# Attention and MLP on one core: the low parts and padded copies of K and V for the second batch pair, moved to later steps

## The chip, the cores and the metric

The kernel runs on one core of a Trainium2 chip. Times are device microseconds (us) of one execution. Engines by their names in the profile: PE is TensorE (matmuls; PEld its weight loads), DVE VectorE, ACT ScalarE, POOL GpSimd, SP SyncE, whose queue issues all the DMAs named here. Every engine works through its own queue in order; an instruction that waits holds everything behind it.

## The reference

Attention with a learned bias of relative position, then an MLP with squared ReLU. Batch 4, 8 heads, sequence 576, head size 64, float32 throughout:

```
scores = q @ k.T / 8 + bias          # bias[h,i,j] = relu(x*w1 + b1) @ w2,
                                     # x = log1p(|i-j|) / log1p(max(i,1))
attn   = softmax(scores)
y      = attn @ v                    # to 2304 tokens x 512
out    = relu(y @ w_in)**2 @ w_out   # 512 -> 2048 -> 512
```

## The kernel before

**Two halves per number.** TensorE multiplies float16. A float32 operand is split into a high part (its value, scaled by a power of two, rounded to float16) and a low part (what the rounding left over, again float16). A product is the sum of three matmuls: high by high, high by low, low by high.

**Tiling.** The four batches make two pairs (`p` = 0, 1). In a pair the rows of the queries are cut into five chunks (`c`): four of 128 rows of each batch and one, c = 0, of the last 64 rows of both. A step is one pair, chunk and head; the chunks come in the order 0, 3, 2, 4, 1 for the first pair and 1, 4, 2, 3, 0 for the second, with eight heads each, so there are 80 steps and the second pair begins at step 40. Step `t` does, in the program's order: `qk` (scores into PSUM), `softmax_a` (line 441: VectorE adds the bias and takes the row maximum; lines 445 and 447: ScalarE's negated maximum and exponential), `softmax_b` (line 129: ScalarE's cast to the high part; lines 473 and 474: GpSimd subtracts to get the low part; line 476: a transposing DMA `at<-a`), and `pv` (line 506), the product with V of the step three before. The buffers `a` and `at` have two slots each.

**The MLP** is work put between the steps. When a chunk has its eight heads, `finish_x` makes eight units of it. In each, `g1` (line 560) is the first product; ScalarE (line 566), VectorE (568 and 133) and GpSimd (570) make its squared ReLU in two parts; `g2` (line 583) is the second product, two units later. `g2` adds up all eight units in the PSUM tiles `o`, which ScalarE evicts at the end (line 590) before the next chunk's first `g2` can write them.

**K and V.** The tiles of the second pair are loaded and split during steps 31 to 43, while the first pair's last chunk and the second pair's first are computed. A load goes through one of three staging buffers `stg` (the MLP's weights have used them before). `split` then makes the high part on GpSimd (line 131), the low part on VectorE (line 191 for K, line 156 for V, one instruction that reads the staged tile and the high part), for K two ScalarE copies (the last 64 rows of the pair's first batch, the first 64 of its second) into the zero-padded tile `kz` (line 196; `qk` reads it), and for V a GpSimd fill of zeros (line 160). The staging buffer is free when the high and low parts are made; the next load into it (line 179) waits for that in SyncE's queue. Splits are at one a step for steps 32 to 35, two for 36 to 39, one for 40 to 43; in order: K 0 to 3, then K 4, V 0, K 5, V 1, K 6, V 2, K 7, V 3, then V 4 to 7. The K tile of head h is read first at step 40 + h, the V tile at step 43 + h.

**What sets the order.** A planner takes the traced instructions, each with a priority (its place in the program, moved by `place`), simulates the engines, and writes out the order of each engine's queue. An instruction goes into a queue at the first moment at which, in that simulation, the engine is free and its inputs are there; among several, the one traced first. A dependency of the kind `NoSync` only tells the planner to put one instruction behind another on the same engine; it makes no semaphore. `behind()` puts such an edge from everything traced in its block to the engine's last pinned instruction, and `pinned` writes out the order at the start.

Of the kernel before, what the change touches and what calls it, by code (L numbers as in the profile page):

```python
# [51 lines left out]
def tile_attention_moe(  # L52
# [96 lines left out]
    def v_split(p, h, st):  # L149
        t = vp.tile([128, 2, 640], F16, tag="v", name="v")  # L150
        cast(zn("vh", p * 8 + h), t[:, 0, :], st, float(2 ** VS))
        if p == 0:
            cast("P", st, st, float(2 ** VS))
            nc.gpsimd.tensor_tensor(t[:, 1, :], st, t[:, 0, :], op=ALU.subtract)
        else:
            nc.vector.scalar_tensor_tensor(
                out=t[:, 1, :], in0=st, scalar=float(2 ** VS), in1=t[:, 0, :],
                op0=ALU.mult, op1=ALU.subtract)

        nc.gpsimd.memset(t[64:128, 1, :].rearrange("p (b j) -> p b j", b=2)[:, :, 256:320], 0.0)  # L160
        v_t[p, h] = t

    class KV:
        def __init__(self, p, h, which):
# [16 lines left out]
        def split(self):  # L181
            st = self.st
            if self.which == "k":
                n = self.p * 8 + self.h
                t = kp.tile([128, 2, S], F16, tag="k", name="k")
                st = st[:, 0:S]
                cast(zn("kh", n), t[:, 0, :], st, float(2 ** KS))
                if zn("kl", n) == "P":
                    nc.gpsimd.tensor_tensor(t[:, 1, :], st, t[:, 0, :], op=ALU.subtract)
                else:  # L190
                    nc.vector.scalar_tensor_tensor(
                        out=t[:, 1, :], in0=st, scalar=float(2 ** KS), in1=t[:, 0, :],
                        op0=ALU.mult, op1=ALU.subtract)
                for b in range(2):
                    r = slice(64 * b, 64 * b + 64)
                    nc.scalar.activation(out=kz[r, n % NKZ, :, r], in_=t[r, :, 512 - 512 * b:576 - 512 * b], func=AF.Copy)
                k_t[self.p, self.h] = t
            elif self.p:
                v_split(self.p, self.h, st[:, 0:640])
# [198 lines left out]

    st_ = {}
    sums = {}  # L400

    def qk(p, c, h):
        kt = k_t[p, h]
# [25 lines left out]
    def softmax_a(p, c, h):  # L429
# [8 lines left out]
        inv = float(2.0 ** -(QS + KS + 3))  # L438
        for b in range(nb):
            sb = b if c else h % 2  # L440
            nc.vector.tensor_tensor_reduce(  # L441
                s[:, 576 * b:576 * b + 576],
                sc[:, 960 * sb:960 * sb + 576], bt, inv, -3.0e38, ALU.add, ALU.max, mx[:, b:b + 1])
        for b in range(nb):
            nc.scalar.activation(out=nm[:, b:b + 1], in_=mx[:, b:b + 1], func=AF.Identity, scale=-1.0, bias=esc)  # L445
            sl = s[:, 576 * b:576 * b + 576]
            nc.scalar.activation(out=sl, in_=sl, func=AF.Exp, bias=nm[:, b:b + 1], accum_out=su[:, h, b:b + 1])  # L447
        st_[p, c, h] = s

    def softmax_b(p, c, h):  # L450
# [271 lines left out]
            pin[i.engine] = i.name  # L722

    @contextmanager
    def behind():
        cur = nc.cur_bb
        n0 = len(cur.bb.instructions)
        yield
        for i in cur.bb.instructions[n0:]:
            if i.engine in pin:  # L730
                tc.add_manual_dep(i, pin[i.engine], mybir.DependencyInfo(
                    mybir.DependencyClass.NoSync, mybir.DependencyReason.DATA), reason="behind")

    pin = {}
    with pinned():
# [27 lines left out]
        hgen(groups[gi])  # L763
        for h in range(2):
            bias_ld(*steps[h])
    with behind():
        kv_load(0, "v")
        ld_dma(ws)
        kv_load(2, "k")
# [7 lines left out]
    for t in range(NS + LAG):  # L777
        now[0] = t
        fence = ExitStack()
        if t < 2:  # L780
            fence.enter_context(behind())
        last = t - LAG
        if t < NS:
            p, c, h = steps[t]
# [32 lines left out]
        with place("kd"):  # L817
            kv_dma(t + 2)
        w_tasks(t + 1)
        for _ in range(nls[t]):  # L820
            ld_split()
            ld_dma(loads2)
# [53 lines left out]
```

## Time and profile before

| | us |
|---|---|
| three runs | 656.75, 657.12, 660.38 (median 657.12) |
| the profiled execution | 661.45 |
| its span, first to last instruction | 659.7 |
| TensorE (PE) busy | 615.1 (93%) |
| VectorE (DVE) busy | 407.1 (62%) |
| ScalarE (ACT) busy | 388.1 (59%) |
| GpSimd (POOL) busy | 376.5 (57%) |
| mean granted TensorE clock | 0.965 |

Starts in the trace count from the beginning of the span. Busy shares are means over the whole span, so what a stage is bound by is read from its own waits and timeline. Granted clock is a share of full speed. In a row, `out<-in` names the tiles, `L191` the line, `x8` a count; `[4.01 <-POOL v L131]` says that the engine stood idle for 4.01 us before the instruction, and that GpSimd's line 131 ended the wait. The chain of waits follows the last end back, at each step to what released it.

### The profile page before, as it was taken

How to read it: one execution, taken by the hardware profiler on the slowest of the kernel's cores; microseconds unless marked ns; L12 is line 12 of the kernel's file. 1: busy time of each engine (PE TensorE's matmuls, PEld its weight loads, DVE VectorE, ACT ScalarE, POOL GpSimd, SP SyncE). 2: the span in 40 equal slices, each digit the busy share in tenths (PEclk: the TensorE clock that was granted, in tenths of full speed). 3: DMA queues.
4: the chain of work that ended last, by engine and by line, in shares of the span. 5: the costliest groups of instructions: out<-in, count | busy, mean ns of one | idle time of the engine just before them, and what ended most of it. 6: DMA issues, size and time to landing. Idle time of an engine off the chain costs nothing.

```text
span 659.7 us, 15574 instructions
## 1 busy us (share of the span) xinstructions
PE 615.1 (93%) x6056; PEld 394.8 (60%) x6056; DVE 407.1 (62%) x813; ACT 388.1 (59%) x856; POOL 376.5 (57%) x394
## 2 busy tenths in 40 slices
PE   5565798999899999999899999999999999999997
PEld 2223356766455566666576676676676676767664
DVE  7997999888864765585856447346545642632321
ACT  5587978788776476656656655656465564342111
POOL 2757578899665456756775465555464663432221
PEclk9698967999999999999899999999999999999999
DMA  7999888477876787889978778679787777524000
GB/s 237 278 294 319 268 255 248 155 209 178 197 173 152 162 193 176 179 180 226 221 170 158 167 134 174 140 169 153 139 172 134 154 149 155 122 56 86 17 34 16
DMA packets 206568, 112.16 MB, mean 170 GB/s; under 512 B 167072, under 2 KB 183456, under 8 KB 206496
## 3 DMA queue, kind: packets, MB, share of 16 engines
q1 hardware_dynamic: 206496, 111.19, 72.0%
q8 instruction: 47, 0.77, 0.5%
q14 instruction: 25, 0.20, 0.1%
HBM read 55.44 MB, written 15.61 MB: 108 GB/s over the span
## 4 chain that ended last, share of the span: by engine, by line
PE 69%; DVE 5%; DMA 4%; issue 2%; ACT 1%; POOL 1%; DVEq 0%; POOLq 0%; ACTq 0%
PE o L583 26%; PE hp L560 26%; PE pv L506 8%; PE sc L425 5%; PE bp L348 2%; DMA at<-a 2%; DVE hg L309 1%; PE sc L419 1%; PE sc L413 1%; DMA xt<-xh 1%; DMA stg<-vd 1%; DVE s L441 1%; DVE cv L226 0%; DVE ci L224 0%; ACT a L129 0%
## 5 line engine op out<-in xcount | busy, mean ns | idle before, releaser
L560 PE MATMUL hp<-xt,winH 128*128 128x256 f16 (+1 forms) x1280 | 195.9, 263 | 0.0
L583 PE MATMUL o<-woutH,g 128*128 128x512 f16 x576 | 185.6, 382 | 4.0 <-ACT o L590 2.2
L560 PE MATMUL hp<-xt,winL 128*128 128x256 f16 (+1 forms) x640 | 162.8, 263 | 0.0
L583 PEld LDWEIGHTS <-g 128*128 128x128 f16 x864 | 82.8, 98 | 97.0 <-issue 11.5
L560 PEld LDWEIGHTS <-winH 128*128 128x128 f16 x1280 | 117.0, 99 | 30.0 <-issue 13.6
L441 DVE CUSTOM_DVE_ANT_0 s<-sc,bt 128x576 f32<-128x576 f32 x144 | 103.5, 751 | 44.1 <-PE sc L425 34.2
L474 POOL TENSOR_TENSOR a<-s,a 128x1024 f16<-128x1024 f32 (+1 forms) x64 | 130.3, 2036 | 0.0
L568 DVE TENSOR_TENSOR r<-hp,r 128x512 f32<-128x512 f32 (+1 forms) x80 | 50.6, 632 | 118.7 <-ACT r L566 118.6
L570 POOL TENSOR_TENSOR g<-r,g 128x512 f16<-128x512 f32 (+1 forms) x80 | 86.7, 1084 | 59.1 <-DVE g L133 48.4
L447 ACT ACTIVATE s<-s,nm 128x576 f32<-128x576 f32 x144 | 111.3, 773 | 6.4
L583 PE MATMUL o<-woutL,g 128*128 128x512 f16 x288 | 109.8, 381 | 0.0
L473 POOL TENSOR_TENSOR a<-s,a 128x128 f16<-128x128 f32 (+1 forms) x64 | 28.1, 440 | 140.4 <-ACT a L129 135.5
L445 ACT ACTIVATE nm<-mx,esc 128x1 f32<-128x1 f32 x144 | 40.9, 288 | 110.8 <-DVE mx L441 110.5
L506 PE MATMUL pv<-v,at 128*128 128x64 f16 (+5 forms) x2112 | 97.9, 207 | 0.5 <-ACT at L460 0.5
L129 ACT ACTIVATE a<-s 128x1152 f16<-128x1152 f32 (+1 forms) x64 | 70.5, 1102 | 44.6 <-DMA at<-a 43.6
L566 ACT ACTIVATE r<-hp 128x512 f32<-128x512 f32 (+1 forms) x80 | 43.1, 539 | 49.6 <-PE hp L560 49.6
L506 PEld LDWEIGHTS <-at 128*128 128x128 f16 (+1 forms) x1792 | 58.3, 100 | 20.2 <-issue 8.6
L560 PEld LDWEIGHTS <-winL 128*128 128x128 f16 x640 | 62.9, 98 | 5.8
L309 DVE TENSOR_SCALAR hg<-tab_t 128x464 f32<-128x464 f32 (+17 forms) x86 | 58.9, 729 | 11.5 <-PE bp L348 11.4
L425 PE MATMUL sc<-k,q 64*128 64x512 f16 x384 | 55.6, 387 | 0.0
L369 ACT ACTIVATE be<-bp,hcst,rows_s 128x288 f32<-128x288 f32 (+29 forms) x67 | 35.8, 571 | 16.5 <-PE bp L348 11.1
L348 PE MATMUL bp<-hg,w2s 128*32 128x288 f32 (+15 forms) x152 | 36.1, 546 | 6.1 <-ACT hg L303 2.4
(88 smaller groups left out, 688.7 us busy)
## 6 DMA issues: line engine op xcount, KB each, us to landing
bt<-biasd SPq DMA_DIRECT2D x64, 288.0 KB, 3.3
stg<-w_in SPq DMA_DIRECT2D x16, 512.0 KB, 5.1
stg<-w_out SPq DMA_DIRECT2D x16, 512.0 KB, 4.7
bt<-biasd SPq DMA_DIRECT2D x32, 144.0 KB, 3.4
qst<-qd SPq DMA_DIRECT2D x32, 128.0 KB, 3.5
out<-o SPq DMA_DIRECT2D x16, 256.0 KB, 2.4
v<-vd SPq DMA_DIRECT2D x8, 320.0 KB, 4.9
stg<-vd SPq DMA_DIRECT2D x8, 320.0 KB, 4.3
```

The lines of the kernel that those rows point to most:

```text
L129: nc.scalar.activation(out=out, in_=in_, func=AF.Copy, scale=scale)
L309: nc.vector.tensor_scalar(ht, src, scl[:, n:n + 1], None, op0=ALU.min)
L348: nc.tensor.matmul(out=bp[32 * t:32 * t + 32, 0:d1 - d0], lhsT=w2s if gi < 4 or PATS[z][t] == "A" else w2n, rhs=ts_[t][:, d0:d1], start=Tr ...
L425: nc.tensor.matmul(out=sc[:, 1024 * b:1024 * b + 512], lhsT=qt[r, qz, qs], rhs=kt[r, z, 64 * b:64 * b + 512], start=(n == 0), stop=(n == 2 ...
L441: nc.vector.tensor_tensor_reduce(s[:, 576 * b:576 * b + 576], sc[:, 960 * sb:960 * sb + 576], bt, inv, -3.0e38, ALU.add, ALU.max, mx[:, b: ...
L447: nc.scalar.activation(out=sl, in_=sl, func=AF.Exp, bias=nm[:, b:b + 1], accum_out=su[:, h, b:b + 1])
L474: nc.gpsimd.tensor_tensor(av[:, :, 640:1152], ev[:, :, 0:512], av[:, :, 0:512], op=ALU.subtract)
L506: nc.tensor.matmul(out=dst, lhsT=lhsT, rhs=vt[r, 5 * b + blk, :] if f32 else vt[:, vz, 5 * b + blk, :], start=(n == 0), stop=(n == nt - 1) ...
L560: nc.tensor.matmul(out=hp[:, f * T:f * T + T].rearrange("p (b t) -> p b t", b=nb), lhsT=wt[:, k, c0:c0 + 128], rhs=xt[:, 0:nb, z * 4 + k, ...
L568: nc.vector.tensor_tensor(rr, hp[:, 0:2 * T], rr, op=ALU.mult)
L570: nc.gpsimd.tensor_tensor(g[:, 1, 0:2 * T], r[:, 0:2 * T], g[:, 0, 0:2 * T], op=ALU.subtract)
L583: nc.tensor.matmul(out=blk["o"][b], lhsT=g[:, z, c0:c0 + 128], rhs=wt[:, 2 * u + f, :], start=(u == 0 and f == 0 and z == 0 and wt is wout ...
```

## The change

Three moves, for the second pair alone (the first pair's K and V are made as before):

- The low part (lines 191 and 156) isn't traced with the high part. It is put on a list, `lo_due`, with the number of the next step, and traced near the end of that step, with a `NoSync` edge behind the step's softmax maximum on VectorE. V's fill on GpSimd goes with it.
- The two copies into `kz` are put on a list, `kz_due`, two steps on, and are traced there behind the step's last exponential on ScalarE.
- `behind` takes the table of last instructions as an argument; `soft` is the table that `softmax_a` fills with the names of its last maximum and last exponential.

```diff
--- before.py
+++ after.py
@@ -153,12 +153,28 @@
             cast("P", st, st, float(2 ** VS))
             nc.gpsimd.tensor_tensor(t[:, 1, :], st, t[:, 0, :], op=ALU.subtract)
         else:
-            nc.vector.scalar_tensor_tensor(
-                out=t[:, 1, :], in0=st, scalar=float(2 ** VS), in1=t[:, 0, :],
-                op0=ALU.mult, op1=ALU.subtract)
+            lo_due.append((now[0] + 1, t, st, VS))
+            v_t[p, h] = t
+            return
 
         nc.gpsimd.memset(t[64:128, 1, :].rearrange("p (b j) -> p b j", b=2)[:, :, 256:320], 0.0)
         v_t[p, h] = t
+
+    lo_due = deque()
+
+    def low_part(t, st, e):
+        nc.vector.scalar_tensor_tensor(
+            out=t[:, 1, :], in0=st, scalar=float(2 ** e), in1=t[:, 0, :],
+            op0=ALU.mult, op1=ALU.subtract)
+        if e == VS:
+            nc.gpsimd.memset(t[64:128, 1, :].rearrange("p (b j) -> p b j", b=2)[:, :, 256:320], 0.0)
+
+    kz_due = deque()
+
+    def kz_copy(n, t):
+        for b in range(2):
+            r = slice(64 * b, 64 * b + 64)
+            nc.scalar.activation(out=kz[r, n % NKZ, :, r], in_=t[r, :, 512 - 512 * b:576 - 512 * b], func=AF.Copy)
 
     class KV:
         def __init__(self, p, h, which):
@@ -188,12 +204,11 @@
                 if zn("kl", n) == "P":
                     nc.gpsimd.tensor_tensor(t[:, 1, :], st, t[:, 0, :], op=ALU.subtract)
                 else:
-                    nc.vector.scalar_tensor_tensor(
-                        out=t[:, 1, :], in0=st, scalar=float(2 ** KS), in1=t[:, 0, :],
-                        op0=ALU.mult, op1=ALU.subtract)
-                for b in range(2):
-                    r = slice(64 * b, 64 * b + 64)
-                    nc.scalar.activation(out=kz[r, n % NKZ, :, r], in_=t[r, :, 512 - 512 * b:576 - 512 * b], func=AF.Copy)
+                    lo_due.append((now[0] + 1, t, st, KS))
+                if self.p:
+                    kz_due.append((now[0] + 2, n, t))
+                else:
+                    kz_copy(n, t)
                 k_t[self.p, self.h] = t
             elif self.p:
                 v_split(self.p, self.h, st[:, 0:640])
@@ -398,6 +413,7 @@
 
     st_ = {}
     sums = {}
+    soft = {}
 
     def qk(p, c, h):
         kt = k_t[p, h]
@@ -438,13 +454,15 @@
         inv = float(2.0 ** -(QS + KS + 3))
         for b in range(nb):
             sb = b if c else h % 2
-            nc.vector.tensor_tensor_reduce(
+            i = nc.vector.tensor_tensor_reduce(
                 s[:, 576 * b:576 * b + 576],
                 sc[:, 960 * sb:960 * sb + 576], bt, inv, -3.0e38, ALU.add, ALU.max, mx[:, b:b + 1])
+            soft[i.ins.engine] = i.ins.name
         for b in range(nb):
             nc.scalar.activation(out=nm[:, b:b + 1], in_=mx[:, b:b + 1], func=AF.Identity, scale=-1.0, bias=esc)
             sl = s[:, 576 * b:576 * b + 576]
-            nc.scalar.activation(out=sl, in_=sl, func=AF.Exp, bias=nm[:, b:b + 1], accum_out=su[:, h, b:b + 1])
+            i = nc.scalar.activation(out=sl, in_=sl, func=AF.Exp, bias=nm[:, b:b + 1], accum_out=su[:, h, b:b + 1])
+            soft[i.ins.engine] = i.ins.name
         st_[p, c, h] = s
 
     def softmax_b(p, c, h):
@@ -722,13 +740,13 @@
             pin[i.engine] = i.name
 
     @contextmanager
-    def behind():
+    def behind(last):
         cur = nc.cur_bb
         n0 = len(cur.bb.instructions)
         yield
         for i in cur.bb.instructions[n0:]:
-            if i.engine in pin:
-                tc.add_manual_dep(i, pin[i.engine], mybir.DependencyInfo(
+            if i.engine in last:
+                tc.add_manual_dep(i, last[i.engine], mybir.DependencyInfo(
                     mybir.DependencyClass.NoSync, mybir.DependencyReason.DATA), reason="behind")
 
     pin = {}
@@ -763,7 +781,7 @@
         hgen(groups[gi])
         for h in range(2):
             bias_ld(*steps[h])
-    with behind():
+    with behind(pin):
         kv_load(0, "v")
         ld_dma(ws)
         kv_load(2, "k")
@@ -778,7 +796,7 @@
         now[0] = t
         fence = ExitStack()
         if t < 2:
-            fence.enter_context(behind())
+            fence.enter_context(behind(pin))
         last = t - LAG
         if t < NS:
             p, c, h = steps[t]
@@ -817,6 +835,12 @@
         with place("kd"):
             kv_dma(t + 2)
         w_tasks(t + 1)
+        while lo_due and lo_due[0][0] <= t:
+            with behind(soft):
+                low_part(*lo_due.popleft()[1:])
+        while kz_due and kz_due[0][0] <= t:
+            with behind(soft):
+                kz_copy(*kz_due.popleft()[1:])
         for _ in range(nls[t]):
             ld_split()
             ld_dma(loads2)
```

## Rows read from the trace of the kernel before

**Rows 1.** the page: busy time, share of the span and instructions of each engine

```profile
PE 615.1 (93%) x6056; PEld 394.8 (60%) x6056; DVE 407.1 (62%) x813; ACT 388.1 (59%) x856; POOL 376.5 (57%) x394
```

**Rows 2.** TensorE's waits, 262 us to the end: total, times, longest (us)

```profile
PE o L583 <- ACT o L590: 2.2, 1, 2.2
```

**Rows 3.** timeline of TensorE: start, duration (us), instruction, [idle before]

```profile
309.88 0.98 PE L506 MATMUL pv<-v,at 128*128 128x64 f16 x28
...
316.70 0.38 PE L583 MATMUL o<-woutH,g 128*128 128x512 f16 x1 [2.19 <-ACT o L590]
```

**Rows 4.** busy us (count) of PE, PEld, DVE, ACT, POOL; granted clock; DMA

```profile
317.00:318.00 1.00, 1.00 (x5) 0.37 (x4) 1.00 (x2) 0.23 (x1) 0.64 (x1) 0.61 0.93 345
...
319.00:320.00 1.00, 1.00 (x3) 0.30 (x2) 1.00 (x5) 0.67 (x2) 1.00 (x3) 0.50 1.07 126
320.00:321.00 1.00, 1.00 (x5) 0.42 (x4) 1.00 (x1) 0.97 (x4) 1.00 (x2) 0.69 1.23 218
```

**Rows 5.** the chain of waits, 255 to 355 us: start, duration (us), what

```profile
299.95 7.64 DMA at<-a
...
312.61 0.70 POOL v L131
...
314.53 0.76 DVE k L191
...
315.96 0.69 ACT o L590
...
316.70 4.44 PE o L583 x12
...
325.60 2.59 PE o L583 x12
```

**Rows 6.** timeline of ScalarE (ACT)

```profile
307.67 1.16 ACT L129 ACTIVATE a<-s 128x1152 f16<-128x1152 f32 x1 [3.74 <-DMA at<-a]
...
313.13 1.16 ACT L129 ACTIVATE a<-s 128x1152 f16<-128x1152 f32 x1 [0.98 <-DMA at<-a]
315.31 0.63 ACT L196 ACTIVATE kz<-k 64x128 f16<-64x128 f16 x2 [1.02 <-DVE k L191]
```

**Rows 7.** timeline of VectorE (DVE), two low parts of V

```profile
304.97 1.28 DVE L156 SCALAR_TENSOR_TENSOR v<-stg,v 128x640 f16<-128x640 f32 x1 [3.16 <-POOL v L131]
...
313.33 1.27 DVE L156 SCALAR_TENSOR_TENSOR v<-stg,v 128x640 f16<-128x640 f32 x1 [4.01 <-POOL v L131]
```

**Rows 8.** waits of all engines, 255 to 350 us

```profile
DVE v L156 <- POOL v L131: 17.9, 6, 4.8
...
DVE k L191 <- POOL k L131: 6.3, 3, 2.6
```

**Rows 9.** timeline of SyncE's DMA queue

```profile
306.27 0.33 SPq L179 DMA_DIRECT2D stg<-kd  x1
306.94 0.33 SPq L179 DMA_DIRECT2D stg<-vd  x1
307.37 3.90 SPq L476 DMA_TRANSPOSE at<-a  x1
```

**Rows 10.** lines 191 and 156 by themselves: ns min/median/max, first and last start

```profile
L191 DVE SCALAR_TENSOR_TENSOR k<-stg,k x8: 741/752/1161, 267.3 to 321.1; 128x576 f16<-128x576 f32 x8
...
L156 DVE SCALAR_TENSOR_TENSOR v<-stg,v x8: 810/1048/1276, 290.5 to 342.3; 128x640 f16<-128x640 f32 x8
```

**Rows 11.** timeline of VectorE: a softmax maximum, and line 544 twice

```profile
270.18 0.75 DVE L441 CUSTOM_DVE_ANT_0 s<-sc,bt 128x576 f32<-128x576 f32 x1
...
454.37 0.75 DVE L544 SCALAR_TENSOR_TENSOR xh<-x,cc,xh 128x512 f16<-128x512 f32 x1
...
461.44 2.50 DVE L544 SCALAR_TENSOR_TENSOR xh<-x,cc,xh 128x512 f16<-128x512 f32 x1
```

**Rows 12.** timeline of GpSimd (POOL): the long subtraction of line 474

```profile
270.75 2.13 POOL L474 TENSOR_TENSOR a<-s,a 128x1024 f16<-128x1024 f32 x1
...
461.07 2.31 POOL L474 TENSOR_TENSOR a<-s,a 128x1024 f16<-128x1024 f32 x1
```

## The prediction

> **What bounds the kernel now.** I began with the busy shares: TensorE is busy for 93% of the span, no other engine for more than 62% [rows 1]. So I asked next where TensorE stands still, and what ends its idle time. From 262 us to the end the view of its waits has one line: once, for 2.19 us, the second product of the MLP (line 583) waited for ScalarE's eviction of the accumulator `o` (line 590) [rows 2]. The timeline shows it: the matmul starts at 316.70, so TensorE stopped at 314.51 [rows 3]. The stop has a second cost. Granted clock is 0.61, 0.50 and 0.69 in the stretches behind it [rows 4], where 0.50 is the 1.2 GHz level and 1.00 the 2.4 GHz one; the 12 matmuls of line 583 that came next took 4.44 us on the chain of waits, where the same 12 took 2.59 us a step later [rows 5]. That is 1.85 us more. Stall and slow clock together: 2.19 + 1.85 = **4.04 us**. Everything else that TensorE does from 262 us to the end runs back to back, so an edit to those steps can give back about 4.0 us and not much more.
>
> Why was `o` late? The chain of waits, read backwards [rows 5]: the eviction began at 315.96, directly behind the padded copy of K (line 196, a pair of 0.63 us on ScalarE's timeline, [rows 6]), which waited for the low part of K on VectorE (314.53). That stood in VectorE's queue behind the low part of V, started at 313.33 after 4.01 us of idle time [rows 7], because GpSimd made the high part of V only from 312.61. So ScalarE was held for 1.02 us in front of the copies [rows 6], and `o`, behind them in a queue kept in order, paid for a K tile that is wanted steps later. The view of waits over 255 to 350 us says how often VectorE does this: 17.9 us in 6 waits for V and 6.3 us in 3 for K [rows 8].
>
> **The change, part by part.** No instruction is added or taken away; 16 low parts, 16 copies (eight pairs) and 8 fills are moved, all between steps 32 and 45 of 80.
>
> *Low parts one step later, behind the maximum.* Eight of K at a median of 752 ns and eight of V at 1048 ns [rows 10]: 6.0 + 8.4 = 14.4 us of VectorE, before and after. What goes are the waits for GpSimd: a high part made one step earlier is finished when the low part's turn comes. That takes 17.9 + 6.3 = 24.2 us of head-of-line waiting out of VectorE's queue [rows 8]. VectorE is not what TensorE waits for, so this is worth nothing by itself; its worth is that the maximum, the squared ReLU and the copies behind it are no longer late.
>
> *What the new place can cost.* The old place was a gap in GpSimd's work, the new one is not: at step 33 the maximum ends at 270.18 + 0.75 = 270.93, and GpSimd's long subtraction for the softmax weights runs from 270.75 for 2.13 us [rows 11, 12]. An operation of the same form (two inputs from SBUF, line 544) took 0.75 us alone and 2.50 us when it met that subtraction [rows 11, 12], 1.75 us more. In the other direction a low part of V that now runs beside a cast may shrink from 1.27 [rows 7] to the least of its line, 0.81 [rows 10]. Bounds for VectorE: between 16 x 1.75 = 28 us more and 4 x 0.46, about 2 us less (four of the eight V parts stand near 1.27). There is one long subtraction in a step, so only the first low part behind a maximum meets it: 12 steps with low parts, 21 us at most. I take half of that, about 11 us, for the two meet in the row I looked at but the planner staggers them. It is less than the 24.2 us of waits that go, so VectorE is not later than now and the term on the path is zero; if it were the whole 28, VectorE would be some 4 us later spread over twelve steps, 0.3 us a step, still nothing on TensorE.
>
> The Trainium skill has a rule that speaks against this part: its page GPSIMD Engine Reference, section 8 (Key points), says that GpSimd shares its SBUF interfaces with VectorE and that VectorE instructions with two SBUF inputs contend with it. The trace agrees, 0.75 against 2.50 us [rows 11]. By the rule alone the edit would make VectorE slower, by the 21 us; by the rows the 24.2 us of waits stand against that. The rule is what keeps rival 2 below alive.
>
> *Copies two steps later, behind the exponentials.* The pair of 0.63 us [rows 6] is ready when ScalarE comes to it, so the 1.02 us of waiting in front of it goes. The copy for another tile (the one of step 36, due at step 38) may now stand in about the same place, 0.63 us of work without a wait. With nothing in front, `o` follows the cast (line 129), which ends at 313.13 + 1.16 = 314.29 [rows 6]: 0.69 us of eviction [rows 5] ends at 314.98, 0.47 us after TensorE stopped. With a copy between, 1.10 us after. But the cast itself had waited 0.98 us for a transpose (at<-a) [rows 6], and that transpose left SyncE at 307.37, behind two loads of V and K issued at 306.27 and 306.94 [rows 9], each 0.02 or so after the low part that frees its staging buffer (the V part of 304.97 + 1.28 = 306.25 [rows 7]). So part of ScalarE's lateness was VectorE's wait as well. Bounds for what is left of the stall: 0 (the cast comes 0.98 us earlier: 314.98 is then 314.00, before TensorE asks) and 1.10 us. I take 0.2, nearer to zero, because both waits in front of the eviction hang on the same late low parts. With so short a stop I let the clock stay up.
>
> *Staging buffers and SyncE.* There are three. A load can be issued when a low part has freed one, and that is now a step later in the program; nothing of K or V is needed soon (the first tile of K is split at step 32 and read at step 40), so late loads cost nothing themselves. Their price is on SyncE, which issues in order: a transpose behind a waiting load leaves late. The V and K loads gain because the low part no longer waits for GpSimd, and lose because it waits for the maximum. I take zero.
>
> *Fills of V's padding* go to GpSimd one step later, behind a low part that is long done; zero, and GpSimd loses some waits.
>
> **Sum.** On the profiled execution's own time, 661.45 us: 661.45 - 4.04 + 0.2 = 657.6. The median of the runs before is 657.12, 4.33 below that execution; I move the same 3.8 us over to it: **653.3 us**. Nothing hides the gain: TensorE has no later wait [rows 2], so what it saves at 316 reaches the end.
>
> **Rivals.**
> 1. *Another wait takes the place of the one removed, or the median run hardly has the stall.* If a copy still precedes `o` and the cast stays where it is, 1.10 us of stall is left, and if the clock falls again, 1.85 more: 2.95 of 4.04 stays, 656.0 us. If the runs around 657 never had the stall, the change does nothing they could show: 657. For it: the runs spread from 656.75 to 660.38 and the profiled one lies above, which fits a stall that comes and goes; against it: the stall follows from the order of the queues, and that order is fixed in the program. The change not doing what it says (the planner, which writes the order of all queues from a simulation, puts the eviction behind something else) ends here too.
> 2. *SyncE's queue becomes the bound (the slower side).* Place: steps 36 to 39, with two loads each. If the planner puts a load ahead of the transpose, the transpose waits for the maximum and two low parts, one of them beside GpSimd's subtraction: 2.50 + 0.75 us. The transpose issued at 299.95 landed at 307.59 [rows 5], where the cast that waits for it starts [rows 6], and TensorE used it at 309.88 [rows 3]: it can be 2.29 us later for nothing. From there on each of four steps stops TensorE; at 2.6 us later that is 0.3 us of stall and 1.85 of slow clock, 4 x 2.15 = 8.6, less the 4.04: 657.12 + 4.6 = 661.7 us. For it: loads already go out the moment a low part ends, with a transpose right behind [rows 9]. Against it: VectorE loses 24.2 us of waits there, and in the trace the same order of transposes behind loads has not stopped TensorE at line 506 [rows 2].
>
> **How the numbers follow.** Forecast 0.46 (own range 652.5 to 654.3), rival 1 with 0.33 (655 to 657.5), rival 2 and other new stops by the planner's reordering 0.21 (657.5 to 663). About 0.5%, 3.3 us, is what a measurement of this kernel tells from no change, so the line lies at 653.8, inside the forecast's own range: of its 0.46 I count 0.39 as faster, 0.07 as same. Rival 1 is same with 0.33; of rival 2, 0.05 is same and 0.16 slower (from 660.4). Faster 0.39, same 0.45, slower 0.16. The range of 8 in 10 leaves out rival 2's worse part and a small tail below: 652.0 to 660.0.
>
> **What would show it.** Right: no wait of line 583 for line 590 near 315 us; granted clock 1.00 from 262 us on; VectorE's waits for GpSimd's high parts (24.2 us) near zero; copies on ScalarE with no idle time before them; some low parts at 1.5 to 2.5 us. Wrong: TensorE waiting in lines 506 (for at) or 560 between 270 and 350 us, SyncE waiting for low parts longer than now, or the same stop with another instruction in front of the eviction.

## The result: 661.80 us, 0.65% slower

The changed kernel took 661.80 us (median of nine runs, 659.80 to 662.83), the kernel before 657.12 us in nine runs beside it. The medians are 4.7 us apart; the ratio, with the scatter of the runs taken into account, is 1.0065, with an interval of 1.0045 to 1.0084, about 4.3 us more. The forecast was 653.3 us with a range that ended at 660.0. Below, a ratio is to the kernel before on the same chip, with the 95% interval in brackets.

Line numbers have moved: the maximum of line 441 is at 457, the exponential at 464, the casts' subtractions at 491 and 492, the transposes at 494, the loads at 195, `pv` at 524, `g1` at 578, `g2` at 601, the eviction of `o` at 608. All low parts of the second pair are on line 166, the copies on line 177. The profiled execution took 661.49 us, a usual one for this kernel.

**The old stop is gone, and a new one is there.** First the busy line of the page (it answers to [rows 1]):

```profile
PE 619.2 (94%) x6056; PEld 398.6 (60%) x6056; DVE 406.0 (62%) x813; ACT 387.9 (59%) x856; POOL 383.3 (58%) x394
```

TensorE's waits from 262 to 360 us (they answer to [rows 2]), in us: total, times, longest:

```profile
PE pv L524 <- DMA at<-a: 2.4, 1, 2.4
```

No wait of `g2` for the eviction of `o` is left. The timeline of ScalarE around the old place (to [rows 6]) shows why: the copies go through with no idle time before them, and the eviction starts at 312.39, where it started at 315.96 before [rows 5].

```profile
308.68 0.61 ACT L177 ACTIVATE kz<-k 64x128 f16<-64x128 f16 x2
...
312.39 1.25 ACT L608 ACTIVATE o<-o,os 128x512 f32<-128x512 f32 x2
```

What stands in its place is a stop of 2.39 us at the `pv` of step 39, whose transposed weights `at` come late. Below, T2 is the transpose that this `pv` waits for, and T1 the transpose before it in SyncE's queue, that of step 38. The timeline of TensorE (to [rows 3]) has the `pv` before it and the late one:

```profile
331.09 0.98 PE L524 MATMUL pv<-v,at 128*128 128x64 f16 x28
...
335.38 1.68 PE L524 MATMUL pv<-v,at 128*128 128x64 f16 x28 [2.39 <-DMA at<-a]
```

The same 28 matmuls took 0.98 and 1.68 us. The stretches of 10 us (to [rows 4]; busy us and count of PE, PEld, DVE, ACT, POOL, then granted clock, DMA share, GB/s) show the clock behind the stop, 0.83 as a mean over 330 to 340 us, and 1.00 around it:

```profile
310.00:320.00 10.00, 10.00 (x122) 6.90 (x121) 6.18 (x11) 6.86 (x14) 9.86 (x9) 1.00 1.01 247
...
330.00:340.00 10.00, 7.61 (x92) 5.65 (x91) 7.70 (x19) 6.58 (x16) 8.78 (x9) 0.83 1.07 215
340.00:350.00 10.00, 10.00 (x90) 6.21 (x89) 8.67 (x12) 5.79 (x12) 7.76 (x10) 1.00 0.72 153
```

**Who made the transpose late.** The chain of waits, 255 to 355 us (to [rows 5]), in order of time; its first two rows here are the usual price of 24 matmuls of `g1` and of one `pv`:

```profile
255.21 2.73 PE hp L578 x24
...
260.52 0.83 PE pv L524 x28
...
324.37 2.26 DVE k L166
326.63 1.70 DVE v L166
328.33 0.46 DVE r L586
328.79 6.55 DMA at<-a
...
335.38 1.68 PE pv L524 x28
337.06 3.47 PE hp L578 x24
```

Two late low parts of VectorE stand in front of the transpose that TensorE waits for. The landing of a DMA is the moment when its data are there; this one landed 6.55 us after its issue. Behind it the slow clock costs (1.68 - 0.83) + (3.47 - 2.73) = 1.6 us; stop and clock together are 4.0 us. The links between VectorE and the transpose are in SyncE's queue (to [rows 9]):

```profile
321.91 1.29 SPq L276 DMA_DIRECT2D qst<-qd  x2
323.30 3.10 SPq L494 DMA_TRANSPOSE at<-a  x1
326.50 0.53 SPq L409 DMA_DIRECT2D bt<-biasd  x1
327.12 1.56 SPq L195 DMA_DIRECT2D stg<-vd  x2
328.79 3.95 SPq L494 DMA_TRANSPOSE at<-a  x1
```

Two loads of V stand between T1 (323.30) and T2 (328.79). Each needs the staging buffer that a low part frees; the second went out when VectorE's low part of V had ended at 326.55 + 1.77 = 328.32, and T2 went out behind it. SyncE stood 0.8 us for that low part. The timeline of VectorE (to [rows 7]) has these low parts, and that of GpSimd what ran beside them:

```profile
321.19 0.69 DVE L283 SCALAR_TENSOR_TENSOR q<-qst,q 128x512 f16<-128x512 f32 x1 [4.36 <-POOL q L131]
...
324.28 2.35 DVE L166 SCALAR_TENSOR_TENSOR k<-stg,k 128x576 f16<-128x576 f32 x1
326.55 1.77 DVE L166 SCALAR_TENSOR_TENSOR v<-stg,v 128x640 f16<-128x640 f32 x1
```

```profile
323.88 2.13 POOL L492 TENSOR_TENSOR a<-s,a 128x1024 f16<-128x1024 f32 x1
325.97 1.67 POOL L588 TENSOR_TENSOR g<-r,g 128x512 f16<-128x512 f32 x1
```

Both low parts lie wholly beside GpSimd's work: 2.35 us against a least of 0.75 for K, 1.77 against 0.82 for V. VectorE's waits for GpSimd's high parts of K and V, 24.2 us before [rows 8], are 2.0 us, in the waits of all engines from 255 to 350 us. But a wait of 4.4 us for the high part of `q` is new; the same view of the kernel before has none:

```profile
DVE q L283 <- POOL q L131: 4.4, 1, 4.4
...
DVE v L166 <- POOL v L131: 2.0, 2, 1.4
```

So the parts of the change do what they say, TensorE's old wait is gone, and the time is longer. That leaves two questions: why the old wait was worth nothing, and which part brings the new one.

### The profile page after: what moved, and what is told of

It reads as the page before. It is cut to its first block, busy times and chain, and to the rows that moved or that the text cites. A ratio compares the mean times of both kernels' runs of the same rounds, so it can differ in the third digit from the quotient of the medians.

```text
span 659.7 us, 15583 instructions
## 1 busy us (share of the span) xinstructions
PE 619.2 (94%) x6056; PEld 398.6 (60%) x6056; DVE 406.0 (62%) x813; ACT 387.9 (59%) x856; POOL 383.3 (58%) x394
## 4 chain that ended last, share of the span: by engine, by line
PE 66%; DVE 4%; DMA 4%; issue 2%; POOL 2%; ACT 2%; SPq 1%; DVEq 0%; POOLq 0%; ACTq 0%
PE hp L578 24%; PE o L601 24%; PE pv L524 8%; PE sc L441 5%; DMA at<-a 3%; PE bp L363 2%; PE sc L435 1%; PE sc L429 1%; DVE hg L324 1%; DVE s L457 1%; DMA stg<-vd 1%; POOL a L492 1%; SPq L494 1%; POOL g L588 1%; ACT a L129 1%
## 5 line engine op out<-in xcount | busy, mean ns | idle before, releaser
L492 POOL TENSOR_TENSOR a<-s,a 128x1024 f16<-128x1024 f32 (+1 forms) x64 | 132.0, 2063 | 0.0
L324 DVE TENSOR_SCALAR hg<-tab_t 128x464 f32<-128x464 f32 (+17 forms) x86 | 53.5, 667 | 12.2 <-PE bp L363 11.9
L363 PE MATMUL bp<-hg,w2s 128*32 128x288 f32 (+15 forms) x152 | 38.0, 587 | 7.5 <-ACT hg L322 2.8
```

What stands on the lines that cost most here:

```text
L324: nc.vector.tensor_scalar(ht, src, scl[:, n:n + 1], None, op0=ALU.min)
L363: nc.tensor.matmul(out=bp[32 * t:32 * t + 32, 0:d1 - d0], lhsT=w2s if gi < 4 or PATS[z][t] == "A" else w2n, rhs=ts_[t][:, d0:d1], start=Tr ...
L492: nc.gpsimd.tensor_tensor(av[:, :, 640:1152], ev[:, :, 0:512], av[:, :, 0:512], op=ALU.subtract)
```

## The experiments

The first theory, A in the expectations: the low parts' new place makes SyncE's loads wait, the transposes behind them are late, and `pv` stops. Its other half says that most executions of the kernel before don't have the old stop. Rivals: the old stop is always there, and the time differs in the steps ahead of it (B); the copies do the harm (C); GpSimd and VectorE slow each other, and `q`'s high part is late on GpSimd (D). Each edit below is against the changed kernel.

### The kernel before, again

The kernel before, with no edit.

> The kernel before against itself, to see a second profile of it. Theory A (the stop of line 583 at 316 us is not in most executions of before, so removing it had nothing to give): the ratio is 1.000 within 0.3%, and if the profiled execution lies near 657 us, its trace has no TensorE wait near 316, or one well under 2.2 us, and granted clock 1.00 there. Rival B (the stop is always there and the 4 us between executions come from the steps before 260 us, which are the same program in both kernels): the trace of an execution near 657 us still shows about 2 us of stop near 312 to 316, and the step at 288.7 us comes 3 to 4 us earlier.

657.24 us, 0.9992 [0.9972, 1.0013]. Its profiled execution took 657.36 us, close to the median, and TensorE's timeline has this instead of [rows 3]:

```profile
313.98 0.38 PE L583 MATMUL o<-woutH,g 128*128 128x512 f16 x1 [0.27 <-ACT o L590]
332.80 0.99 PE L506 MATMUL pv<-v,at 128*128 128x64 f16 x28 [0.22 <-DMA at<-a]
```

The stop of 2.19 us that the prediction removes is one of 0.27 us in this execution, and the granted clock is 1.00 in all of 290 to 350 us. The eviction of `o` began at 313.24 behind a copy that did not wait. SyncE's queue, with T1 at 321.72 and T2 at 326.43, has its loads ahead of T1:

```profile
318.66 1.54 SPq L179 DMA_DIRECT2D stg<-vd  x2
320.34 1.28 SPq L261 DMA_DIRECT2D qst<-qd  x2
321.72 3.90 SPq L476 DMA_TRANSPOSE at<-a  x1
325.72 0.53 SPq L394 DMA_DIRECT2D bt<-biasd  x1
326.43 3.29 SPq L476 DMA_TRANSPOSE at<-a  x1
```

From the first scores of step 33 to those of step 44 this execution took 78.39 us, the changed kernel's 81.78: 3.39 us, near the 2.39 - 0.22 - 0.27 + 1.6 = 3.5 us of stops and clock. The rest of the program is the same in both, and the loss is in these steps. In the first profile of before they took 81.64 us, so 3.25 us of what set that execution apart lie here. Rival B is out: step 33 began at 268.37 us there and at 267.57 us here, only 0.80 us earlier.

A single profile has a limit, though. What stands ahead of step 33 is the same program in every kernel here, and it took 264.61 to 270.08 us in the thirteen profiles; what follows the first scores of step 44 took 309.7 to 309.8 us, and 310.3 us with the loads spread. So the whole time of one execution doesn't say what its steps 33 to 44 took, and these steps are set beside the ratios in the table below.

### The copies late, the low parts as before

```diff
-            lo_due.append((now[0] + 1, t, st, VS))
-            v_t[p, h] = t
-            return
+            nc.vector.scalar_tensor_tensor(
+                out=t[:, 1, :], in0=st, scalar=float(2 ** VS), in1=t[:, 0, :],
+                op0=ALU.mult, op1=ALU.subtract)
...
-                    lo_due.append((now[0] + 1, t, st, KS))
+                    nc.vector.scalar_tensor_tensor(
+                        out=t[:, 1, :], in0=st, scalar=float(2 ** KS), in1=t[:, 0, :],
+                        op0=ALU.mult, op1=ALU.subtract)
```

> Only the copies into the padded tile are two steps late; low parts stay where they were, and VectorE's and SyncE's orders are those of before. Theory A with its second half (after is slow because late low parts free the staging buffers late, SyncE stands at the loads, and the transpose behind them comes late for pv near 333 us): no wait of pv for a transpose over 0.5 us, time that of before or up to 4 us less, 653 to 657 us, ratio 0.994 to 1.000. Rival C (the late copies do the harm, as 0.6 us of ScalarE in front of the ReLU and the cast in eight steps): 660 to 662 us, ratio about 1.007, with the stop of about 2.4 us near 333 as in after.

657.56 us, 0.9995 [0.9976, 1.0015]. The largest stop is 0.80 us (`g2` for the eviction of `o`), `pv` waits 0.35 us. The copies' move costs nothing and brings nothing that can be measured; rival C is out.

### The low parts late, the copies right behind them

```diff
-                    lo_due.append((now[0] + 1, t, st, KS))
-                if self.p:
-                    kz_due.append((now[0] + 2, n, t))
-                else:
+                    lo_due.append((now[0] + 1, t, st, KS, n))
+                if not self.p:
                     kz_copy(n, t)
...
+            x = lo_due.popleft()
             with behind(soft):
-                low_part(*lo_due.popleft()[1:])
+                low_part(*x[1:4])
+            if len(x) > 4:
+                kz_copy(x[4], x[1])
```

> Low parts one step late behind the maximum as in the changed kernel, but each pair of copies right after its low part, in the same step and with no edge; VectorE's, GpSimd's and SyncE's orders are those of the changed kernel. Theory A: as slow as the changed kernel, 660 to 662.5 us, ratio 1.005 to 1.009, pv waits 2 to 2.5 us for a transpose near 333 us. Rival C (the copies do it): near 657 us, ratio about 1.000.

661.58 us, 1.0047 [1.0021, 1.0073]. `pv` stops for 3.39 us at the same place, more than the 2 to 2.5 expected, with a granted clock of 0.83 in 330 to 340 us. The low parts alone bring the loss, within the two intervals the whole of it.

### Five staging buffers instead of three

The change as it is, with two more buffers, taken from the pool of the bias tables.

```diff
+    nst = [-1]
...
-                self.st = stg_p.tile([128, 1024], F32, tag="stg", name="stg")
+                nst[0] += 1
+                self.st = (hg_p.tile([128, 1152], F32, tag="w", name="hg") if nst[0] % 5 > 2 else
+                           stg_p.tile([128, 1024], F32, tag="stg", name="stg"))
```

> The changed kernel, but K and V of the second pair go through five staging buffers, the three of before and two that the bias tables have done with. Theory A: loads no longer stand in SyncE's queue in front of the transposes until a low part has ended, so the transpose for step 39 is issued before 328 us and pv's wait near 333 is under 1 us: 656 to 658.5 us, ratio 0.998 to 1.003. Rival D (the transposes are late because GpSimd and VectorE slow each other and q's split is late, not for want of buffers): the wait near 333 stays at 2 us or more and the time at 660 us or above, ratio 1.005 or more.

658.54 us, 1.0004 [0.9981, 1.0026]: the loss in time is gone, as A has it. The profiled execution (658.00 us) was not as expected, though. In SyncE's queue T2 goes out 4.41 us behind T1, with a load between that waited for nothing:

```profile
320.95 3.13 SPq L498 DMA_TRANSPOSE at<-a  x1
...
324.80 0.37 SPq L199 DMA_DIRECT2D stg<-vd  x1
325.36 4.07 SPq L498 DMA_TRANSPOSE at<-a  x1
```

and yet `pv` stopped for 1.65 us where less than 1 was expected, and the scores of another step for 1.54 us, for a maximum behind the low part of `q`, which had waited 5.43 us for GpSimd:

```profile
323.67 0.33 PE L439 MATMUL sc<-kz,q 128*128 128x128 f16 x3 [1.54 <-DVE mx L461]
333.46 0.99 PE L528 MATMUL pv<-v,at 128*128 128x64 f16 x28 [1.65 <-DMA at<-a]
```

The clock stayed at 1.00 behind both. Steps 33 to 44 took 81.02 us here, 2.6 us more than in the kernel before, again, while the ratio shows a loss of 0.3 us and at most 1.7. This execution made up for it ahead of step 33, which began at 265.53 us. Whether most executions of this kernel have these stops can't be known from one profile.

### K's low parts late alone, and V's alone

K late, V as before:

```diff
-            lo_due.append((now[0] + 1, t, st, VS))
-            v_t[p, h] = t
-            return
+            nc.vector.scalar_tensor_tensor(
+                out=t[:, 1, :], in0=st, scalar=float(2 ** VS), in1=t[:, 0, :],
+                op0=ALU.mult, op1=ALU.subtract)
```

> The changed kernel with V's low parts put back (made with their high part, no edge); K's low parts and the copies stay late. Theory A says a load behind a late low part stands in front of the transpose for step 39: K's loads are all out by then and only V's are left, so most of the loss goes: pv waits under 1 us near 333, ratio 0.999 to 1.003. Rival D (GpSimd's work is stretched by low parts that run beside it, K's first of all, and the cast of q comes late): half the low parts still stretch it, ratio 1.003 or more and pv waits 1.5 us or more.

666.24 us, 1.0158 [1.0135, 1.0181], the worst of all. Theory A gave 1.003 at most; D allowed a larger loss, but with `pv` as the one that waits. TensorE stands in front of the scores for 5.6 us in four waits and once for `o`, and never at `pv`; granted clock is 0.91 in 290 to 310 us and 0.83 in 330 to 340. Its waits, 262 to 360 us:

```profile
PE sc L435 <- DVE mx L457: 5.6, 4, 2.4
PE o L601 <- ACT o L608: 0.7, 1, 0.7
```

The queues run into each other here. V's low part is still ahead of the next maximum in VectorE's queue and waits for V's cast, which waits for V's load. On GpSimd and on VectorE:

```profile
301.77 0.72 POOL L131 TENSOR_SCALAR v<-stg 128x640 f16<-128x640 f32 x1 [4.80 <-DMA stg<-vd]
```

```profile
302.53 1.04 DVE L156 SCALAR_TENSOR_TENSOR v<-stg,v 128x640 f16<-128x640 f32 x1 [2.74 <-POOL v L131]
303.49 0.74 DVE L457 CUSTOM_DVE_ANT_0 s<-sc,bt 128x576 f32<-128x576 f32 x1
```

The scores that needed this maximum started at 304.98 after 1.94 us of stop. That load went out at 297.85 and waited for no low part: in SyncE's queue it stood behind a transpose of 3.39 us and a load of bias. A later load of V did wait for a buffer; it went out at 306.20, when K's low part, started at 304.85 for 1.32 us, had ended. Why such a chain stops the scores here, and doesn't in the kernel before, was not followed further. The other half is the mirror, V late, K as before:

```diff
-                    lo_due.append((now[0] + 1, t, st, KS))
+                    nc.vector.scalar_tensor_tensor(
+                        out=t[:, 1, :], in0=st, scalar=float(2 ** KS), in1=t[:, 0, :],
+                        op0=ALU.mult, op1=ALU.subtract)
```

> The counterpart: K's low parts put back, V's stay late with the edge (copies late too). Theory A: the loads of V 5 to V 7 wait for late low parts as in the changed kernel, a load stands between the transposes of steps 38 and 39, pv waits 1.5 to 3 us near 333, ratio 1.003 to 1.008. Rival D: GpSimd is stretched by about half, ratio between 1.000 and 1.004.

661.11 us, 1.0061 [1.0041, 1.0082]: stops of 1.67 us at `pv`, 0.98 at the scores, 0.79 for `o`, and no drop of the clock in the profiled execution (659.44 us). Either half alone is as bad as both or worse.

### The high part of `q` from GpSimd to VectorE

```diff
-    "wh": "AAAAAAAA", "wl": "PPPPPPPP", "qh": "PPPDDP",
+    "wh": "AAAAAAAA", "wl": "PPPPPPPP", "qh": "PPPDDDP",
```

> The changed kernel with the high part of q on VectorE instead of GpSimd for the two splits of steps 42 and 46; SyncE's order is that of the changed kernel. In the changed kernel VectorE stood 4.4 us for GpSimd's cast of q, and the load of the next q, ahead of the transpose for step 38, waited for it. Rival D: this is the cause, so pv's wait near 333 falls under 0.8 us and the ratio to 0.999 to 1.002. Theory A: the loads behind the late low parts stay in the queue, so pv still waits 1.2 us or more, ratio 1.002 to 1.007.

662.09 us, 1.0076 [1.0056, 1.0096]; `pv` stops for 2.59 us, the clock stays at 1.00. Rival D alone is out: without the wait for `q`'s high part on GpSimd the loss is as large. The profile shows only part of it, for steps 33 to 44 took 80.32 us, 1.9 us more than in the kernel before, again, where the ratio has 5.0 us; the rest of this execution's time lies ahead of step 33, which began at 270.08 us.

### The loads spread, one in a step

The change as it is, but the second pair's splits at one a step for steps 32 to 47, instead of two a step for 36 to 39.

```diff
-    nls = [0] * 32 + [1] * 4 + [2] * 4 + [1] * 4 + [0] * 50
+    nls = [0] * 32 + [1] * 16 + [0] * 46
```

> The changed kernel with one load and split of K or V in each of steps 32 to 47 instead of two in steps 36 to 39. A slot of the three is then free a step before the next load wants it. Theory A: no load stands at a late low part, pv waits under 0.8 us near 333, ratio 0.996 to 1.002. Rival D: fewer low parts per step also ease GpSimd, so it cannot tell A from D by its time; what tells is whether the loads on SyncE start at the end of a low part (D allows it, A does not).

657.94 us, 1.0013 [0.9997, 1.0029]. TensorE's only wait from 262 to 360 us:

```profile
PE sc L435 <- DVE mx L457: 0.4, 1, 0.4
```

Steps 33 to 44 took 77.66 us, the shortest of all. With the loads spread, the late low parts do no harm that can be measured. The number of loads between T1 and T2 doesn't decide it by itself: there is one here, and one with V late, where the ratio is 1.0061.

### The changed kernel, again

The changed kernel, with no edit.

> The changed kernel once more, for a second profile of it and more of its times. If the late low parts hold the transpose for step 39 in every execution (theory A), its trace has one wait of pv for a transpose of 2 to 3 us near 333 us with 1 to 2 us of slow clock behind it, steps 33 to 45 take 3 us or more longer than in the second profile of before, and the ratio is 1.005 to 1.008. If that was an accident of the one execution seen, the wait is under 1 us.

661.83 us, 1.0069 [1.0048, 1.0090]. The stop is there again, somewhat longer than the 2 to 3 us expected, in TensorE's timeline and in the stretch behind it (columns as above):

```profile
334.77 1.68 PE L524 MATMUL pv<-v,at 128*128 128x64 f16 x28 [3.26 <-DMA at<-a]
```

```profile
334.00:341.00 7.00, 6.22 (x52) 4.93 (x53) 5.52 (x12) 4.43 (x8) 6.38 (x9) 0.52 0.85 200
```

The clock is at its lower level, 1.2 GHz, for nearly the whole 7 us, and half of the 6.22 us of matmuls is what that cost, about 3 us. Steps 33 to 44 took 84.09 us, 5.70 more than in the kernel before, again. The mean of 3.39 and 5.70 is 4.5 us, about the 4.3 that the ratio gives.

### Five staging buffers and `q` on VectorE; early low parts and spread loads

The edits for five staging buffers and for the high part of `q` together:

> The changed kernel with five staging buffers and the high part of q on VectorE for steps 42 and 46. With five buffers alone two stops of 1.54 us (the scores of step 40 wait for a maximum that stood behind q's low part, which waited 5.4 us for GpSimd's cast) and 1.65 us (pv for a transpose) were left. Theory A with rival D as its remainder: the first stop goes (under 0.4 us), the second shrinks under 1 us, ratio 0.997 to 1.001. If the cast of q is not what held the maximum, the 1.5 us stay and the ratio is about that of five buffers alone, 1.000 to 1.003.

656.21 us, 0.9996 [0.9974, 1.0017]: the stop at the scores went, as expected; `pv` still stopped for 2.16 us, where less than 1 was expected. And the copies-late kernel with the spread loads:

> Low parts where they were before, copies two steps late, loads spread to one a step over steps 32 to 47. If what is left in before is only the eviction behind copies and the crowded steps 36 to 39, TensorE has no wait over 0.4 us from 180 to 650 us, the scatter to 660 us goes, and the ratio is 0.995 to 0.999; if before has nothing of that in most executions, 0.998 to 1.002.

658.62 us, 1.0021 [1.0003, 1.0040], stops of 0.98 at `pv`, 0.80 for `o`, 0.45 at the scores, where no wait over 0.4 us was hoped for. No version beats the kernel before: the lowest ratios of a changed program are 0.9995 (copies late) and 0.9996, and both intervals hold 1.

### What the stop at `pv` is made of

Each profiled execution gives three stretches from the timelines of SyncE and TensorE: from T1's issue to the moment when TensorE comes to the `pv`; from T1's issue to T2's; from T2's issue to the start of the `pv`. The stop is the second and third less the first. The last column is the time from the first scores of step 33 to those of step 44.

| kernel | loads between T1 and T2 | T1 to TensorE there | T1 to T2 | T2 to `pv` | stop | steps 33 to 44 |
|---|---|---|---|---|---|---|
| before, first profile | 0 | 11.56 | 4.49 | under 7.07 | 0 | 81.64 |
| before, again | 0 | 10.86 | 4.71 | 6.37 | 0.22 | 78.39 |
| copies late | 0 | 10.36 | 4.41 | 6.30 | 0.35 | 79.48 |
| early low parts, spread | 0 | 10.39 | 5.07 | 6.30 | 0.98 | 80.53 |
| changed | 2 | 9.69 | 5.49 | 6.59 | 2.39 | 81.78 |
| changed, again | 2 | 9.25 | 4.93 | 7.58 | 3.26 | 84.09 |
| low parts late | 2 | 9.41 | 4.95 | 7.85 | 3.39 | 83.32 |
| `q` on VectorE | 2 | 10.56 | 5.02 | 8.13 | 2.59 | 80.32 |
| V late | 1 | 10.34 | 4.83 | 7.18 | 1.67 | 81.42 |
| five staging | 1 | 10.86 | 4.41 | 8.10 | 1.65 | 81.02 |
| five staging, `q` | 1 | 11.02 | 5.02 | 8.16 | 2.16 | 79.82 |
| loads spread | 1 | 11.75 | 4.48 | under 7.27 | 0 | 77.66 |
| K late | 1 | 13.02 | 4.62 | under 8.40 | 0 | 88.29 |

So theory A holds in part. In the changed kernel T1 itself is 1.17 us nearer to TensorE than before (10.86 - 9.69): it stands behind `qst`, which waited for VectorE's low part of `q`, and that for GpSimd. T2 is 0.78 us further behind T1; this is theory A's own term, the loads that wait for low parts. And T2's data take 0.22 us longer: 2.17 us together, the difference of the two stops. In its second execution the same three are 1.61, 0.22 and 1.21. With `q` on VectorE most of the first term is gone (10.56), as rival D has it, and yet the stop stayed, by the third. Five staging buffers took away the first two terms and not the third, which is why 1.65 us was left there.

The third term goes with the loads at this one transpose: with no load between, T2 is used 6.30 to 6.37 us after its issue, with one or two 6.59 to 8.16. The load just ahead moves its data at the same time; in the changed kernel the second one landed 4.4 us after its issue, when T2 was 4.0 us old. A part can be seen on SyncE: T2's row there lasts 3.25 to 3.36 us with no load between and 3.62 to 5.20 us with one or two. That the load is the whole reason is argued and not shown, and another transpose speaks against it: in the kernel before, again, the one issued at 298.12 us, 0.43 us behind a load, landed 5.9 us after its issue, sooner than any T2 without a load.

The Trainium skill, page DMA: Bandwidth & Descriptors, section Queues, rings and completion order, says that each DMA engine takes the descriptors of a ring in the order in which they were put there. By that rule the loads that SyncE issues ahead of the transpose are taken up before it. No row here shows the order inside a DMA engine, and the transpose of 298.12 us shows that such loads alone don't settle the time.

What is shown by the times is this: the late low parts bring the loss, the copies don't, and it goes when there are more staging buffers or when the loads are spread. How much of it each of the three terms is worth in most executions is open, since one profile shows a loss 2.4 us larger than its ratio does (five staging) and another one 3.1 us smaller (`q` on VectorE).

## Why the prediction was wrong

**The step that failed first: "I move the same 3.8 us over to it".** The 4.04 us of stop and clock were read rightly in the profiled execution, and the change does remove them, but that execution, 661.45 us, lay 4.33 us above the median, and they were most of what made it so: steps 33 to 44 took 81.64 us in it and 78.39 in the second profile. The kernel before, again, has 0.27 us there, and the copies-late kernel, whose copies no longer wait for a low part, gains nothing: 0.9995. Of the 80 executions of the kernel before that ran beside the experiments, one took longer than that one. The 3.8 us should have stayed at nothing. In the second profile the cast in front of the eviction had its transpose in time: the cast and the copy ran without waiting, and `o` was free 0.3 us late. The transpose issued at 299.95, which stands in the old chain, had taken 7.64 us to land [rows 5]; the one of that step took 5.9 us in the second profile. So the order of the queues, fixed as it is, doesn't fix the stop. Rival 1 had said this as one of its two ways, for the reason that turned out right, with 0.33.

**The step that failed second: "Staging buffers and SyncE. ... I take zero."** This is the term that was mis-sized. Steps 33 to 44 took 3.4 us more in one execution and 5.7 in another; with five staging buffers the ratio falls from 1.0065 to 1.0004, so 4.0 of the 4.3 us hang on the buffers. The working saw that "a transpose behind a waiting load leaves late", and that loads lose because the low part waits for the maximum; it set the gain of lost GpSimd waits against that without a row for either. What it left out is that VectorE would come to the low part of `q` and wait there, with a load and T1 behind it in SyncE's queue, and that a transpose can be used later even where the load ahead of it waited for nothing (8.10 us with five buffers). Rival 2 had the mechanism (loads, late transposes, TensorE stopping at `pv` with the clock behind it) and the stretch. It had four stops of 2.15 us less the 4.04, and came to 661.7; the two traces have one stop, of 2.39 and of 3.26 us, with 1.6 and about 3 us of slow clock, and nothing to set against it. That its time is the measured one is a coincidence of two errors; its mechanism is not.

**VectorE's contention, "about 11 us" with nothing on the path.** In 255 to 350 us the low parts went from 14.8 to 17.1 us on VectorE (6.4 + 8.4 to 8.9 + 7.4 for seven of V's and 0.8 for the eighth, right behind that stretch): 2.3 us, not 11. Most first low parts do not meet the long subtraction, with a median of 0.80 us for K. The rule of the Trainium skill (GPSIMD Engine Reference, section 8, Key points) holds where they meet, 2.35 against 0.75 us. GpSimd is slowed too, which I counted nowhere. GpSimd's largest group and its casts of V and K, before and after, in 255 to 350 us (busy us, mean ns; one more of the long subtractions falls in the stretch after, so the means are to be compared):

```profile
L474 POOL TENSOR_TENSOR a<-s,a 128x1024 f16<-128x1024 f32 x13 | 27.9, 2145 | 0.0
...
L131 POOL TENSOR_SCALAR v<-stg 128x640 f16<-128x640 f32 x8 | 5.8, 725 | 2.0 <-DMA stg<-vd 2.0
L131 POOL TENSOR_SCALAR k<-stg 128x576 f16<-128x576 f32 x8 | 5.5, 693 | 0.0
```

```profile
L492 POOL TENSOR_TENSOR a<-s,a 128x1024 f16<-128x1024 f32 x14 | 31.4, 2244 | 0.0
...
L131 POOL TENSOR_SCALAR v<-stg 128x640 f16<-128x640 f32 x8 | 7.5, 934 | 7.7 <-DMA stg<-vd 7.6
L131 POOL TENSOR_SCALAR k<-stg 128x576 f16<-128x576 f32 x8 | 6.8, 853 | 0.0
```

Over the whole span GpSimd is busy 383.3 - 376.5 = 6.8 us longer. This by itself isn't the loss: it is busy 383.6 us with five buffers and 384.6 us with the spread loads, as long as in the changed kernel, and neither loses time that can be measured (1.0004, 1.0013).

**What was right.** VectorE's waits for the high parts of K and V went from 24.2 to 2.0 us and were worth nothing by themselves. The copies have no idle time before them, the old stop does not occur, some low parts take 1.7 to 2.4 us. And the rows named as proof against the forecast are the ones that came: TensorE waiting for `at` between 270 and 350 us, SyncE's loads behind low parts.

**What stays open.** A version in which only the edge to the maximum is left away was not run: traced a step later without it, the low parts come out in the same place of VectorE's and SyncE's queues as in the copies-late kernel, so it would have tried nothing new; it is the edge, not the later place in the program, that moves them. Why T2 takes 8.1 us behind one load in the five-buffer kernels and 6.59 behind two in the first execution of the changed kernel is not settled, nor why the median of five buffers shows none of the stops in its profile. Every variant has one profile.

## What to carry to other kernels

Before a stop is priced from a trace, look for it in a second execution, over the same steps. The distance of the profiled execution from the median is a first hint that the stop is that execution's alone, as here, but no more than a hint: executions also differ where the programs are the same, and the kernel with five buffers and `q` on VectorE had a stop of 2.16 us in an execution that lay 0.36 us below its median. When the reader of a staging buffer moves, follow the buffer's release into the issuing queue: every transfer behind the next load moves with it. Moving half of a chain of readers can be worse than moving all: the half that stays can still wait at the head of its queue, with what TensorE needs behind it.

## What the runs showed of the hardware

- GpSimd and VectorE slow each other. In the kernel with K late, the long subtraction that met low parts of V and of K (from 302.85) took 2.71 us, and one beside which no low part ran (from 336.72) 2.13; a cast of V beside a low part took 1.33 us (from 331.80), others 0.72. Which of the two pays differs: in the changed kernel the low part of K at 324.28 took 2.35 us while the subtraction it met kept its 2.13, and the low part of V at 315.79 took 1.04 us while the subtraction that started behind it, at 316.11, took 2.71. I had put the price on VectorE alone.
- A stop of some 2 us may or may not bring TensorE's clock down. In these profiles the granted clock fell behind stops of 1.94, 2.19, 2.39, 2.42, 3.26 and 3.39 us; behind 1.54, 1.65, 1.67, 2.16 and 2.59 us it stayed at 1.00. The length of the stop alone does not decide it. Where it fell, the price was 1.6 to 1.9 us behind the stops of 2.19 and 2.39 us, about 3 us behind that of 3.26, so that the same program loses 3.4 us in one execution and 5.7 in the next.
- The same transpose, at the same place of the same program, was used 6.59 us after its issue in one execution and 7.58 in another.
